# 56 constant matmuls for 30, and another order of the opening, in a kernel of chunk-selected attention and a gated FFN

## The chip, the cores and the metric

The kernel runs on one core of a Trainium2 chip. The metric is the device time of one execution in microseconds (us), lower is better. The engines are named as the profile names them: PE is TensorE's matmuls and PEld its weight loads, DVE is VectorE, ACT is ScalarE, POOL is GpSimd, and SP is the sync engine, which here only issues DMAs.

## The reference

Attention comes first: 4 batches, 8 heads, 768 positions, head size 64. The keys of a head are cut into 24 chunks of 32. For each query and chunk an upper bound is the sum over the head's dimensions of the larger of q times the chunk's minimum and q times its maximum. Each query keeps its six chunks with the highest bound among those that causality allows, and takes a softmax over the causal positions in them. The result is laid out as 3072 tokens of 512 values and goes through a gated feed-forward part with 1536 inner columns.

```python
k_min, k_max = min and max of k over each chunk of 32
ub = sum_d max(q * k_min, q * k_max)           # causal chunks only
top_chunks = argsort(ub)[..., -6:]
scores = q @ k.T / sqrt(64)                    # selected chunks, causal
x = softmax(scores) @ v                        # 3072 x 512
out = (sigmoid(x @ w_gate) * (x @ w_val)) @ w_out
```

## The kernel before

The 3072 tokens are worked in eight units u0 to u7 of three blocks of 128 tokens, 384 columns each. Unit u0 holds the first block of batches 0, 1 and 2; the others hold later blocks. In a first block no chunk has to be chosen, so it goes the short way of the function `first`.

Nothing is scheduled at run time. Every piece of work is put into a plan under a name (`plan.add`), and `Plan.order` replays a string written out by hand, `ORDER`: `kfT_0=P` means that the piece kfT_0 comes next and runs on TensorE (P), and A, V, G and S stand for ScalarE, VectorE, GpSimd and SP. So the string gives both the engine of each piece and the order on each engine. `SLOTS` says which buffer of a kind each tile takes (eight PSUM banks; six "v" buffers for what SP loads first), and `TIES` adds waits between two pieces that share no data. A piece waits only for its data, its buffer and its ties.

The names that matter below, with the unit or block as a suffix:

- `fl_i` (L591, in `keep_awake`): a constant matmul, ones times ones, 128x128 by 256 columns; nothing reads its result. L595 makes 30 of them.
- `kf`, `qf`, `vf` of blocks 0, 1 and 2 are loaded by SP in the function `load_first` (L631, L636). All of them take "v" buffers, so the later ones wait until an earlier one has been read. `kq_u1` is the load of unit u1 (L647).
- `kfT`, `qfT` (L709): the four transposes of a block's keys or queries; `kf16`, `qf16` copy the result to fp16. `scf` (L746): the scores of a block, eight matmuls. `expf` (L751, ScalarE): exponential, one for each half of the heads. `cmf` (L753, GpSimd): causal mask. `pvf` (L760): product with the values, `v16` or `vh` (cast by `vc` on GpSimd). `rzf`, `xf` (L766, L768, VectorE): division by the sum. `xpsf` (L775) turns the result back and `xTf` copies it into `xT_u0`, from which the FFN reads.
- `kn`, `qn` copy the keys and queries of u1 out of their load, `kT`, `qT` (L795) turn them, `kt`, `hk`, `hq`, `qf`, `qm`, `kx`, `kcr` prepare the selection from them, `ub_u1` (L896) computes its bounds.
- `epat` (L566, GpSimd) is a mask pattern for the selection, and the eight `hkp` copies spread it over the rows of the key tiles that hold no keys, 64x1536 values each. Before, three of them are on ScalarE (110, 000, 111), three on VectorE (001, 011, 101), two on GpSimd (010, 100).
- `wgp`, `wg0` to `wg2`, `wv0` to `wv2` (L610 to L613) and `wo0` to `wo2` (L618): the weights in thirds, their DMAs issued by GpSimd. `wgp` is the first quarter of the first third of w_gate, `wg0` the rest of it.
- `g_u0_fb`, `v_u0_fb` (both L1259): gate and value products of unit u0 for 128 inner columns, four matmuls each. fb 0 to 3 read the first third of the weights, 4 to 7 the second, 8 to 11 the last. `g_u0_0` needs all of `xT_u0`.

The hand-over to the later work is smooth: the first score tiles of u1 (`sc_u1`, L957) stand behind the first value products of u0 in TensorE's order, and from there attention of one unit and FFN of the one before alternate.

Of the kernel before, what the change touches and what calls it, by code (L numbers as in the profile page):

```python
# [116 lines left out]
tanh_u0_6=A g_u0_7=P tanh_u0_7=A hg_u0_7=V v16_0_1=G cm_u1_3=G pv_u1_3=P cm_u1_2=G hk1_u1_1=G g_u0_4=P tanh_u0_4=A hg_u0_4=V
vf1_3=G hq1_u1_2=G pv_u1_2=P sc_u1_5_1=P sc_u1_4_2=P sc_u1_4_1=P rz_u1_1=V x_u1_1=V exp_u1_4_1=A v_u0_9=P v_u0_10=P xps_u1_1=P
xT_u1_1=A exp_u1_4_2=A hg_u0_6=V hk1_u1_3=V hg_u0_5=V v_u0_8=P g_u0_10=P tanh_u0_10=A kcr1=V hg_u0_10=V g_u0_8=P tanh_u0_8=A
hg_u0_8=V sc_u1_5_2=P exp_u1_5_2=A g_u0_9=P tanh_u0_9=A hg_u0_9=V sc_u1_4_0=P exp_u1_4_0=A cm_u1_1=G pv_u1_1=P cm_u1_0=G qn_u2_2=G  # L120
sc_u1_5_0=P pv_u1_0=P exp_u1_5_0=A sc_u1_6_1=P exp_u1_6_1=A sc_u1_6_2=P exp_u1_6_2=A exp_u1_5_1=A sc_u1_7_2=P sc_u1_7_0=P
g_u0_11=P qT_u2_2=P sc_u1_7_1=P tanh_u0_11=A exp_u1_7_2=A exp_u1_7_0=A exp_u1_7_1=A kn_u2_1=V kT_u2_1=P rz_u1_0=V x_u1_0=V
xps_u1_0=P cm_u1_5=G pv_u1_5=P cm_u1_4=G pv_u1_4=P qf_u2_2=V q1_u2=S qn_u2_1=V qT_u2_1=P sc_u1_6_0=P kt_u2_1=A exp_u1_6_0=A
kn_u2_0=G kT_u2_0=P kt_u2_0=A v_u0_11=P rz_u1_2=V xT_u1_0=V x_u1_2=V xps_u1_2=P q3_u2=S qn_u2_3=G qT_u2_3=P cm_u1_7=G pv_u1_7=P
kx0_u2_0=V o0_u0_0=P o1_u0_0=P hg_u0_11=V kx1_u2_1=V kx1_u2_0=V cm_u1_6=G pv_u1_6=P rz_u1_3=V x_u1_3=V q0_u2=S qn_u2_0=A qT_u2_0=P
o0_u0_1=P xps_u1_3=P xT_u1_3=V qf_u2_1=A hq0_u2_2=A qf_u2_3=A qm_u2_1=G hq1_u2_1=G k2_u2=S kn_u2_2=G hk1_u2_0=A xT_u1_2=A
kT_u2_2=P k3_u2=S kn_u2_3=A kT_u2_3=P qf_u2_0=V hq0_u2_1=G hq0_u2_0=G qm_u2_0=G hk0_u2_1=G o2_u0_0=P osb_u0_0=A hq1_u2_0=A
qm_u2_2=A qf0_3=S qfT_3=P o1_u0_1=P o2_u0_1=P vf_3=S kf1_3=S kf0_3=S kfT_3=P v_0_5=S v_0_4=S kx0_u2_1=V kx0_u2_3=V kx1_u2_3=V
# [1328 lines left out]
```

## Time and profile before

| what | value |
|---|---|
| runs | 282.29, 280.89 and 280.53 us, median 280.89 |
| profiled execution | 279.88 us, its span 278.2 us |
| busy share of the span | PE 97%, DVE 83%, ACT 65%, POOL 59% |
| moved by DMA | 34.70 MB, mean 125 GB/s |
| granted TensorE clock over the span | 1.00 |

The span runs from the first to the last instruction; some 1.7 us of the execution lie outside it. In the timelines a row is a run of instructions of one kind on one engine: start, length, line, operation, output and inputs, count, and in brackets the idle time before it with what ended it. In the list of waits the numbers are the microseconds in total, how often, and the longest. In the table by stage each engine has its busy time and, in brackets, its number of instructions.

### The profile page before, as it was taken

How to read it: one execution, taken by the hardware profiler on the slowest of the kernel's cores; microseconds unless marked ns; L12 is line 12 of the kernel's file. 1: busy time of each engine (PE TensorE's matmuls, PEld its weight loads, DVE VectorE, ACT ScalarE, POOL GpSimd, SP SyncE). 2: the span in 40 equal slices, each digit the busy share in tenths (PEclk: the TensorE clock that was granted, in tenths of full speed). 3: DMA queues.
4: the chain of work that ended last, by engine and by line, in shares of the span. 5: the costliest groups of instructions: out<-in, count | busy, mean ns of one | idle time of the engine just before them, and what ended most of it. 6: DMA issues, size and time to landing. Idle time of an engine off the chain costs nothing.

```text
span 278.2 us, 7566 instructions
## 1 busy us (share of the span) xinstructions
PE 269.2 (97%) x2806; PEld 189.3 (68%) x2806; DVE 231.2 (83%) x686; ACT 180.4 (65%) x386; POOL 163.1 (59%) x262
## 2 busy tenths in 40 slices
PE   5979999999999999999999999999999999999995
PEld 3755658667755666557687657776888688778684
DVE  4799747687999998796999987978889998888985
ACT  6388969569858944468689979988983422341430
POOL 5797744639372873534669966724766467163440
PEclk9999999999999999999999999999999999999999
DMA  6999999999999598696896230100320033000304
GB/s 157 258 281 204 207 217 208 220 179 202 187 217 189 142 183 188 145 161 125 164 157 114 68 85 17 40 0 3 73 77 2 1 83 127 2 1 2 151 2 152
DMA packets 131717, 34.70 MB, mean 125 GB/s; under 512 B 119776, under 2 KB 128736, under 8 KB 131680
## 3 DMA queue, kind: packets, MB, share of 16 engines
q1 hardware_dynamic: 126912, 29.50, 50.6%
...
## 4 chain that ended last, share of the span: by engine, by line
PE 87%; DMA 6%; DVE 5%; SPq 1%; issue 0%; POOL 0%; DVEq 0%
PE v_u L1259 20%; PE g_u L1259 15%; PE sc_u L957 12%; PE o_u L1308 11%; PE p_u L1082 10%; PE pv_u L990 7%; DMA wg<-in_moe_w_gate_dram 5%; PE p_g_u L1191 5%; PE ube_u L896 3%; DMA kf<-in_k_dram 1%; DVE xf L768 1%; PE kfT L709 1%; PE qfT L709 1%; PE fl L591 1%; DVE kx_u L681 1%; DVE kcr L681 1%
## 5 line engine op out<-in xcount | busy, mean ns | idle before, releaser
L968 ACT ACTIVATE att_u<-sc_u 128x512 f16<-128x512 f32 (+3 forms) x184 | 86.9, 573 | 8.6 <-PE sc_u L957 7.3
L1259 PE MATMUL v_u<-xT_u,wv 128*128 128x384 f16 x384 | 72.4, 326 | 0.0
L1280 DVE SCALAR_TENSOR_TENSOR hg_u<-gate_u,v_u 128x384 f16<-128x384 f16 x96 | 51.2, 545 | 19.3 <-ACT gate_u L1271 9.7
L1271 ACT ACTIVATE gate_u<-g_u 128x384 f16<-128x384 f32 x72 | 35.1, 499 | 40.3 <-PE g_u L1259 35.1
L1259 PE MATMUL g_u<-xT_u,wg 128*128 128x384 f16 x288 | 56.0, 326 | 0.9 <-ACT xT_u L452 0.5
L1259 PEld LDWEIGHTS <-wv 128*128 128x128 f16 x384 | 36.2, 98 | 20.3 <-issue 0.2
L974 POOL TENSOR_SCALAR_AFFINE_SELECT att_u<-att_u 128x384 f16<-128x384 f16 (+1 forms) x56 | 28.0, 509 | 37.4 <-ACT att_u L968 16.4
L1259 PEld LDWEIGHTS <-wg 128*128 128x128 f16 x288 | 26.7, 98 | 18.3 <-DMA wg<-in_moe_w_gate_dram 1.8
L1308 PE MATMUL o_u<-wo,hg_u 128*128 128x512 f16 x144 | 34.3, 379 | 0.0
L990 PE MATMUL pv_u<-v,att_u 128*128 128x65 f16 x640 | 26.3, 193 | 0.0
L990 PEld LDWEIGHTS <-att_u 128*128 128x128 f16 x640 | 24.2, 98 | 2.9 <-issue 0.6
L1228 DVE TENSOR_TENSOR f_g_u<-p_g_u,f_g_u 128x192 f32<-128x192 f32 (+1 forms) x72 | 24.9, 383 | 1.0 <-PE p_g_u L1191 0.4
L957 PE MATMUL sc_u<-hqe,hke 128*128 128x128 f16 (+2 forms) x220 | 25.1, 243 | 0.0
L957 PE MATMUL sc_u<-hqo,hko 128*128 128x128 f16 (+2 forms) x220 | 24.1, 243 | 0.0
L1308 PEld LDWEIGHTS <-hg_u 128*128 128x128 f16 x144 | 13.7, 98 | 13.4
L957 PEld LDWEIGHTS <-hke 128*128 128x128 f16 x220 | 16.5, 98 | 4.9 <-issue 0.6
L957 PEld LDWEIGHTS <-hko 128*128 128x128 f16 x220 | 16.4, 98 | 4.4
L673 POOL CAST v<-v 128x512 f16<-128x512 f32 x23 | 14.4, 627 | 5.8 <-DVE qf_u L863 1.8
L1271 ACT ACTIVATE gate_u<-f_g_u 128x384 f16<-128x384 f32 x24 | 11.9, 519 | 5.6 <-DVE hg_u L1280 2.9
L1011 DVE TENSOR_TENSOR x_u<-pv_u,rz_u 128x384 f16<-128x384 f32 (+1 forms) x28 | 14.6, 524 | 0.9 <-DMA xT_u<-x_u 0.6
L919 DVE MAX8 mx_u<-ubn_u 128x8 f32<-128x8 f32 (+16 forms) x152 | 12.7, 158 | 0.3
L1099 DVE SCALAR_TENSOR_TENSOR sw<-p_u,sw 128x256 f32<-128x256 f32 (+1 forms) x20 | 10.6, 528 | 2.4 <-PE p_u L1082 2.0
...
## 6 DMA issues: line engine op xcount, KB each, us to landing
...
k<-in_k_dram SPq DMA_DIRECT2D x12, 384.0 KB, 5.4
q<-in_q_dram SPq DMA_DIRECT2D x12, 384.0 KB, 5.9
...
wv<-in_moe_w_val_dram POOLq DMA_DIRECT2D x3, 512.0 KB, 9.8
wo<-in_moe_w_out_dram POOLq DMA_DIRECT2D x3, 512.0 KB, 17.6
qf<-in_q_dram SPq DMA_DIRECT2D x8, 128.0 KB, 3.3
```

The costliest lines, as they stand in the source:

```text
L673: plan.add(f"v16_{b}_{ib}", {POOL: pool(H * D)}, lambda e: nc.gpsimd.tensor_copy(v16[b % 2][:, ib, :, 0:D], at(t)), reads=[t], writes=[("v ...
L957: nc.tensor.matmul(at(t)[:, o:o + 128 * m], hk[b % 2][e_][:, p, 128 * jb:128 * jb + 128], hq[u.side][e_][:, p, 128 * x:128 * (x + m)], sta ...
L968: plan.add(f"exp_{u.name}_{h}_{y}", {ACT: act(n)}, lambda e, t=t, att=att, b0=b0, n=n: nc.scalar.activation(at(att)[:, b0:b0 + n], at(t), ...
L974: nc.gpsimd.affine_select(out=dv, in_=dv, compare_op=ALU.is_ge, fill=0.0, base=0, pattern=[[0, u.m], [1, 128]], channel_multiplier=-1)
L990: nc.tensor.matmul(at(pv)[:, last, x, :], at(att)[:, c:c + 128], v16[b % 2][:, jb, h, :], start=(jb == 0), stop=(jb == ib))
L1011: plan.add(f"x_{u.name}_{p}", {DVE: dve(u.t)}, lambda e: nc.vector.tensor_tensor(at(x_).rearrange("p a (e d) -> p e a d", e=2), at(pv)[:, ...
L1082: nc.tensor.matmul(at(to)[:, side], a(j)[:, i], b(j)[:, i], start=j == i == 0, stop=j == 2 and i == 1)
L1228: plan.add(f"{p}_{name}", {POOL: pool2(192 * n), DVE: dve(192 * n)} if slow else {DVE: dve(192 * n)}, lambda e: both(e).tensor_tensor(dst( ...
L1259: nc.tensor.matmul(at(t), w16[:, c, 128 * fb:128 * fb + 128], at(u.xt)[:, c, :], start=(c == 0), stop=(c == 3))
L1271: plan.add(f"tanh_{u.name}_{fb}", {ACT: act(T, not seven[0])}, lambda e, gv=gv, gate=gate: nc.scalar.activation(at(gate), gv(), AF.Tanh, s ...
L1280: plan.add(f"hg_{u.name}_{fb}", {DVE: dve(T)}, lambda e, vv=vv, gate=gate, hg=hg, fb=fb: nc.vector.scalar_tensor_tensor(at(hg)[:, fb % 2], ...
L1308: nc.tensor.matmul(at(o), at(hgs[fc // 2])[:, fc % 2, 128 * tb:128 * tb + 128], wo16[:, fc, lo:hi], start=(fc == 0), stop=(fc == NFB - 1))
```

## The change

The loop makes 56 constant matmuls for 30. The string `ORDER` is another one ahead of `sc_u1_3_0`; from there on, 1765 pieces stand in the same order on the same engines. In the new part

- 32 constant matmuls stand on TensorE ahead of `kfT_0`, where 9 stood, and `kT_u1_2` comes behind `kfT_0`;
- `scf_1` stands behind `pvf_0_1`, and `scf_2` behind `pvf_1_0`;
- four pattern copies are on ScalarE (011, 010, 000, 001), three on VectorE (100, 110, 101), one on GpSimd (111);
- `hkf0` goes from GpSimd to ScalarE, some casts and copies of u1 change their engine, and `cmf_2_0` comes ahead of `wv0` on GpSimd;
- SP issues its 128 DMAs in the same order as before.

Six ties are new. `SLOTS` names other PSUM banks and other buffers of equal kind in much of the kernel; the later pieces keep their waits but for a few that wait for another of the banks just freed.

```diff
--- before.py
+++ after.py
@@ ORDER: all up to the common rest @@
-ident=G ones16=V fl_4=P fl_2=P fl_8=P fl_3=P fl_1=P fl_0=P fl_29=P k2_u1=S kn_u1_2=A qf1_0=S kf1_0=S kf0_0=S fl_6=P fl_5=P epat0=V
-ident16=V ap0=V epat=G hkp110=A hkp000=A hkp001=V kT_u1_2=P kcr0=V kt_u1_2=V hk0_u1_2=G vf1_1=G hkp011=V hkp010=G vf1_2=G hkp100=G
-kf1_2=S kf0_1=S kfT_0=P kxf1=V fl_17=P fl_10=P fl_7=P kx0_u1_2=V kf16_0=V qf0_0=S qfT_0=P qf16_0=V qf1_1=S kf1_1=S kfT_1=P
-kf16_1=V fl_15=P fl_16=P scf_0=P expf_0_1=A fl_19=P qf0_1=S qfT_1=P hq0=V ap1=V fl_14=P fl_9=P fl_13=P fl_11=P fl_18=P fl_12=P
-qf16_1=V scf_1=P v10=G vf_0=S v16_0_0=G qf0_2=S qf1_2=S kf0_2=S expf_0_0=A cmf_0_0=G pvf_0_0=P rzf_0_0=V xf_0_0=V kx1_u1_2=V
-cmf_0_1=G wgp=G kfT_2=P pvf_0_1=P qfT_2=P qf16_2=V rzf_0_1=V xf_0_1=V kxf0=V expf_1_0=A cmf_1_0=G vf_1=S vc_1=G pvf_1_0=P
-rzf_1_0=V xpsf_0_0=P expf_1_1=A cmf_1_1=G pvf_1_1=P hkf0=G hk1_u1_2=A kf16_2=A scf_2=P expf_2_1=A expf_2_0=A k0_u1=S kn_u1_0=V
-kT_u1_0=P xf_1_0=V fl_20=P fl_21=P wg0=G q3_u1=S qn_u1_3=A q2_u1=S rzf_1_1=V xf_1_1=V xpsf_1_1=P hq1=V xTf_1_1=V kx0_u1_0=V
-kx1_u1_0=V vf_2=S wv0=G cmf_2_0=G fl_23=P xpsf_0_1=P fl_24=P fl_22=P fl_27=P xpsf_1_0=P vc_2=G xTf_1_0=V pvf_2_0=P rzf_2_0=V
-xf_2_0=V q1_u1=S k3_u1=S kn_u1_3=G kT_u1_3=P hkp111=A q0_u1=S fl_28=P kx1_u1_3=V cmf_2_1=G pvf_2_1=P xpsf_2_0=P rzf_2_1=V xf_2_1=V
-qT_u1_3=P qf_u1_3=V k1_u1=S qn_u1_1=A qT_u1_1=P xTf_0_0=A xTf_0_1=A qn_u1_2=A qn_u1_0=A kn_u1_1=G kT_u1_1=P kx1_u1_1=V kx0_u1_1=V
-kt_u1_0=A qm_u1_3=A fl_25=P xpsf_2_1=P fl_26=P qT_u1_2=P v_0_3=S v_0_2=S v_0_1=S qf1_3=S k0_u2=S q2_u2=S k1_u2=S qf_u1_1=V
-qf_u1_2=V v11=G wv1=G wg1=G hq0_u1_3=G qT_u1_0=P kt_u1_3=A hk0_u1_3=G hq1_u1_3=G wv2=G xTf_2_1=A xTf_2_0=A qf_u1_0=A qm_u1_0=A
-g_u0_0=P g_u0_2=P kx0_u1_3=V kcr_f=V kcr_u1=V hkp101=V hq1_u1_0=V hkf1=V kt_u1_1=V hk0_u1_1=G wg2=G qm_u1_2=A qm_u1_1=A ub_u1=P
-ubn0_u1=V ubm0_u1=V hq0_u1_1=A hq0_u1_2=A g_u0_3=P g_u0_1=P mx0_u1=V ap0_u1=V apt0_u1=V hqm0_u1_0=V v_u0_1=P v_u0_0=P v_u0_2=P
-hq0_u1_0=A tanh_u0_2=A tanh_u0_1=A hg_u0_1=V ubn1_u1=V v_u0_3=P tanh_u0_3=A hg_u0_3=V ubm1_u1=V hg_u0_2=V tanh_u0_0=A hg_u0_0=V
-hk0_u1_0=A hq1_u1_1=A sc_u1_0_2=P exp_u1_0_2=A sc_u1_1_2=P sc_u1_0_1=P sc_u1_0_0=P exp_u1_1_2=A sc_u1_1_0=P sc_u1_1_1=P
-exp_u1_0_0=A exp_u1_0_1=A v_u0_7=P wo0=G hqm0_u1_2=G sc_u1_2_2=P exp_u1_2_2=A sc_u1_2_0=P exp_u1_2_0=A
+ident=G vf1_1=G ones16=V fl_2=P fl_15=P fl_34=P k2_u1=S hq1=V epat0=V epat=G hkp111=G hkp100=V hkp011=A hkp010=A ident16=V qf1_0=S
+kf1_0=S kf0_0=S fl_8=P fl_19=P fl_53=P fl_28=P fl_10=P fl_32=P fl_40=P fl_30=P fl_13=P fl_48=P fl_26=P fl_27=P fl_31=P fl_33=P
+fl_3=P fl_5=P fl_6=P fl_0=P fl_37=P fl_4=P fl_41=P fl_17=P fl_12=P fl_50=P fl_9=P fl_35=P fl_54=P fl_45=P fl_29=P kfT_0=P
+kn_u1_2=V fl_24=P fl_47=P kT_u1_2=P v10=G hkp000=A kf1_2=S kf0_1=S qf0_0=S qfT_0=P qf16_0=A qf1_1=S kf1_1=S fl_11=P fl_46=P
+fl_23=P fl_51=P qf0_1=S kfT_1=P kf16_0=V kcr0=V fl_18=P scf_0=P fl_7=P fl_43=P fl_38=P qfT_1=P fl_16=P fl_1=P hkp110=V kxf1=V
+qf16_1=V vf_0=S v16_0_0=G qf0_2=S qf1_2=S kt_u1_2=A hk0_u1_2=G expf_0_0=A cmf_0_0=G fl_21=P fl_36=P fl_44=P pvf_0_0=P rzf_0_0=V
+xf_0_0=V kx0_u1_2=V qfT_2=P qf16_2=V fl_14=P fl_52=P xpsf_0_0=P expf_0_1=A vf1_2=G cmf_0_1=G pvf_0_1=P kf16_1=A scf_1=P expf_1_0=A
+kf0_2=S fl_22=P rzf_0_1=V ap0=V kfT_2=P kf16_2=V ap1=V xf_0_1=V xTf_0_0=V fl_25=P fl_39=P fl_20=P wgp=G vf_1=S vc_1=G expf_1_1=A
+hkp001=A cmf_1_0=G pvf_1_0=P scf_2=P expf_2_0=A cmf_1_1=G pvf_1_1=P rzf_1_1=V k0_u1=S kn_u1_0=V kT_u1_0=P wg0=G q3_u1=S q2_u1=S
+fl_42=P vf_2=S cmf_2_0=G wv0=G qn_u1_3=A qT_u1_3=P xf_1_1=V xpsf_1_1=P expf_2_1=A rzf_1_0=V xf_1_0=V kxf0=V xpsf_1_0=P xpsf_0_1=P
+vc_2=A pvf_2_0=P qf_u1_3=A qm_u1_3=A q1_u1=S k3_u1=S kn_u1_3=V kT_u1_3=P q0_u1=S rzf_2_0=V xf_2_0=V hkf0=A xpsf_2_0=P xTf_2_0=A
+qn_u1_1=A xTf_0_1=A cmf_2_1=G pvf_2_1=P fl_55=P kx1_u1_2=V qT_u1_1=P xTf_1_1=A k1_u1=S v_0_3=S v_0_2=S v_0_1=S qf1_3=S k0_u2=S
+q2_u2=S k1_u2=S qn_u1_0=G qT_u1_0=P fl_49=P kn_u1_1=G kT_u1_1=P kt_u1_1=A qn_u1_2=G wv1=G wg1=G wv2=G rzf_2_1=V xf_2_1=V qT_u1_2=P
+qf_u1_2=A qf_u1_1=A qm_u1_2=G kcr_f=G qf_u1_0=A hq1_u1_3=A qm_u1_0=A kx0_u1_3=V kx0_u1_0=V kt_u1_3=V kx1_u1_3=V xTf_1_0=V
+xpsf_2_1=P xTf_2_1=V g_u0_0=P g_u0_2=P kx1_u1_0=V kx0_u1_1=V kx1_u1_1=V kcr_u1=V hkp101=V hk0_u1_1=V hkf1=V hq0_u1_2=V wg2=G
+qm_u1_1=A hk1_u1_2=A ub_u1=P ubn0_u1=V ubm0_u1=V mx0_u1=V kt_u1_0=A hq0_u1_0=G v11=G g_u0_1=P g_u0_3=P ap0_u1=V hq1_u1_0=V
+apt0_u1=V hqm0_u1_0=V hq0=V v_u0_1=P tanh_u0_1=A hg_u0_1=V ubn1_u1=V v_u0_3=P v_u0_0=P v_u0_2=P tanh_u0_3=A hg_u0_3=V ubm1_u1=V
+tanh_u0_2=A hg_u0_2=V tanh_u0_0=A hq0_u1_1=A hg_u0_0=V hk0_u1_0=A hq1_u1_1=A sc_u1_0_2=P exp_u1_0_2=A sc_u1_1_2=P sc_u1_0_1=P
+sc_u1_0_0=P exp_u1_1_2=A sc_u1_1_0=P sc_u1_1_1=P exp_u1_0_0=A exp_u1_0_1=A v_u0_7=P wo0=G hq0_u1_3=G hqm0_u1_2=G sc_u1_2_2=P
+exp_u1_2_2=A sc_u1_2_0=P exp_u1_2_0=A hk0_u1_3=G
 sc_u1_3_0=P ...
@@ SLOTS: the constant matmuls and the renamed banks @@
-epat:0 fl_0:5 fl_1:4 fl_2:1 fl_3:3 fl_4:0 fl_5:0 fl_6:7 fl_7:5 fl_8:2 fl_9:6 fl_10:4 fl_11:3 fl_12:6 fl_13:7 fl_14:3 fl_15:0
...
+epat:0 fl_0:4 fl_1:5 fl_2:0 fl_3:1 fl_4:6 fl_5:2 fl_6:3 fl_7:1 fl_8:3 fl_9:3 fl_10:7 fl_11:5 fl_12:1 fl_13:3 fl_14:5 fl_15:1
...
@@ TIES: six more, the others as they were @@
+hkp111<epat0 qn_u1_0<rzf_2_0 kn_u1_1<xf_2_0 qn_u1_2<kx1_u1_2 qm_u1_2<xf_2_1 hq0_u1_0<hq0_u1_2
...
-    for i in range(30):
+    for i in range(56):
         keep_awake(i)
```

More of the change, by code (lines that the diff above doesn't have):

```diff
@@ L117 @@
[L117 to L128, printed above, removed]
@@ L264 @@
+c21_u7=V out_u7_1=S out_u7_0=S held_u6_5=A p2z_u67=P p6_u67=P p6z_u67=P p5_u67=P p5z_u67=P c11_u67=V u4_u67=V sw3_u67_2=G
+sw3_u67_1=G p3_u67=P p3z_u67=P c12_u67=V out_u67_0=S sw2_u67_2=G p7_u67=P p7z_u67=P c22_u67=V out_u67_b1=S p4_u67=P p4z_u67=P
+c21_u67=V out_u67_1=S
 """
 SLOTS = """
[L267 to L268 removed]
@@ L269 @@
-vf_0:5 kf_1:3 qf_1:4 vf_1:0 kf_2:2 qf_2:1 vf_2:3 kq_u1:0 v_0_1:2 v_0_2:5 v_0_3:4 kfT_0:2 kf16_0:3 kx_f:0 qfT_0:6 qf16_0:4
-scf_0_0:4 scf_0_1:5 attf_0_0:1 pvf_0_0:5 rzf_0_0:0 xf_0_0:0 xpsf_0_0:5 xT_u0:0 attf_0_1:2 pvf_0_1:6 rzf_0_1:1 xf_0_1:1 xpsf_0_1:1
-kfT_1:7 kf16_1:5 qfT_1:0 qf16_1:6 vh_1:1 scf_1_0:7 scf_1_1:3 attf_1_0:3 pvf_1_0:7 rzf_1_0:0 xf_1_0:2 xpsf_1_0:7 attf_1_1:1
-pvf_1_1:3 rzf_1_1:1 xf_1_1:0 xpsf_1_1:0 kfT_2:4 kf16_2:4 qfT_2:0 qf16_2:0 vh_2:2 scf_2_0:1 scf_2_1:0 attf_2_0:3 pvf_2_0:0
@@ new lines @@
+kq_u1:0 v_0_1:1 v_0_2:5 v_0_3:4 kfT_0:0 kf16_0:3 kx_f:0 qfT_0:4 qf16_0:2 scf_0_0:6 scf_0_1:7 attf_0_0:1 pvf_0_0:6 rzf_0_0:0
+xf_0_0:0 xpsf_0_0:5 xT_u0:0 attf_0_1:2 pvf_0_1:7 rzf_0_1:1 xf_0_1:1 xpsf_0_1:2 kfT_1:2 kf16_1:1 qfT_1:1 qf16_1:4 vh_1:0 scf_1_0:2
+scf_1_1:6 attf_1_0:3 pvf_1_0:2 rzf_1_0:1 xf_1_0:0 xpsf_1_0:5 attf_1_1:1 pvf_1_1:1 rzf_1_1:0 xf_1_1:2 xpsf_1_1:1 kfT_2:1 kf16_2:2
+qfT_2:4 qf16_2:5 vh_2:6 scf_2_0:6 scf_2_1:4 attf_2_0:2 pvf_2_0:4 rzf_2_0:0 xf_2_0:2 xpsf_2_0:6 attf_2_1:3 pvf_2_1:4 rzf_2_1:1
@@ new lines @@
+xf_2_1:0 xpsf_2_1:2 kn_u1_0:1 kT_u1_0:7 kx_u1:1 kt_u1_0:0 kn_u1_1:1 kT_u1_1:1 kt_u1_1:1 kn_u1_2:1 kT_u1_2:3 kt_u1_2:0 kn_u1_3:2
+kT_u1_3:0 kt_u1_3:2 qn_u1_0:0 qT_u1_0:6 qf_u1:0 qm_u1:0 qn_u1_1:5 qT_u1_1:3 qn_u1_2:4 qT_u1_2:4 qn_u1_3:4 qT_u1_3:6 ube_u1:2
+ubo_u1:4 ubn_u1:0 mx_u1:0 apt_u1:0 g_u0_0:0 gate_u0_0:0 v_u0_0:2 hg_u0_0:0 g_u0_1:3 gate_u0_1:2 v_u0_1:1 g_u0_2:5 gate_u0_2:1
+v_u0_2:3 hg_u0_1:1 g_u0_3:6 gate_u0_3:3 v_u0_3:7 g_u0_4:6 gate_u0_4:0 v_u0_4:5 hg_u0_2:3 g_u0_5:4 gate_u0_5:2 v_u0_5:2 g_u0_6:1
@@ new lines @@
+k16_2_3<kx0_2_0 v16_2_0<hg_u2_0 k16_2_1<rz_u3_3 hk0_2_0<x_u3_1 v16_2_1<qf1_u4_0 hq0_u4_2<qm_u4_2 hq0_u4_0<qf0_u6_1
+hq1_u4_0<qf0_u6_3 kcr_2<hg_u2_11 hk0_2_2<mx1_u4 cm_u4_1<qf0_u5_2 cm_u4_2<hg_u3_0 k16_3_2<qf0_u6_2 qm_u5_2<k16_3_0 cm_u4_7<kt_3_1
+cm_u4_3<hqm0_u5_0 cm_u4_5<rz_u4_0 hq0_u5_2<hg_u3_6 v16_2_2<hg_u3_7 v16_2_4<rz_u4_1 hqm0_u5_2<x_u4_1 cm_u4_6<kx0_3_2
+hk0_3_1<rz_u4_2 cm_u5_0<x_u4_2 k16_3_3<rz_u4_3 hqm1_u5_0<x_u4_3 v16_3_0<qf1_u6_2 hqm1_u5_2<rz_u5_0 cm_u5_3<qf1_u6_3 hk1_3_1<kt_3_3
+hq0_u7_2<hk0_3_3 cm_u5_5<qf0_u7_1 v16_3_2<x_u5_1 hq0_u7_0<ubn1_u6 hqm1_u6_2<hqm1_u6_0 v16_2_5<rz_u5_2 cm_u6_3<x_u5_2
```

476 lines of the change are left out of this document (239 added, 237 removed).

## The prediction

> **What bounds the kernel now.** First the page, for the share of each engine and the chain that ended last.
>
> ```profile
> PE 269.2 (97%) x2806; PEld 189.3 (68%) x2806; DVE 231.2 (83%) x686; ACT 180.4 (65%) x386; POOL 163.1 (59%) x262
> PEclk9999999999999999999999999999999999999999
> DMA  6999999999999598696896230100320033000304
> PE 87%; DMA 6%; DVE 5%; SPq 1%; issue 0%; POOL 0%; DVEq 0%
> ```
>
> TensorE is busy in 97% of the span, so nearly everything it must do sets the end, and only its idle time or its useless work can be won. The DMA row is full in the first 13 of 40 slices: during the change's part of the kernel, something else runs at its limit too. The second view is TensorE's waits, the third the chain of waits.
>
> ```profile
> PE fl L591 <- DVE ones L587: 1.1, 1, 1.1
> PE pvf L760 <- POOL vh L456: 1.0, 2, 0.8
> PE kfT L709 <- DMA kf<-in_k_dram: 0.9, 1, 0.9
> PE kT_u L795 <- POOL epat L566: 0.8, 1, 0.8
> PE g_u L1259 <- ACT xT_u L452: 0.5, 1, 0.5
> PE g_u L1259 <- DMA wg<-in_moe_w_gate_dram: 0.2, 1, 0.2
> ```
> ```profile
> 26.18 14.22 DMA wg<-in_moe_w_gate_dram
> 40.45 1.48 PE g_u L1259 x8
> ```
>
> These six waits make 4.5 us of the whole execution, and every one lies before 40.5 us. The chain says more than the length of a wait does: the last thing it finds ahead of TensorE's unbroken run is no work of the opening but the third part of w_gate, issued at 26.18 and landed at 26.18 + 14.22 = 40.40. TensorE stood ready only 0.25 us earlier. So 40.40 is a meeting point of two streams, and the change touches both: TensorE's opening and the time at which GpSimd issues the weights. To know how close they run I read the traffic by stage, then the landings of single weight parts.
>
> ```profile
> 5.00:10.00 5.00, 4.19 (x21) 3.02 (x23) 3.84 (x7) 1.78 (x2) 4.12 (x7) 1.00 1.07 241
> 15.00:20.00 5.00, 3.72 (x47) 2.53 (x46) 4.65 (x16) 3.85 (x8) 4.85 (x9) 1.00 1.19 292
> 20.00:25.00 5.00, 4.37 (x48) 2.95 (x52) 4.92 (x14) 4.92 (x14) 4.05 (x8) 1.00 1.22 204
> 35.00:40.00 5.00, 5.00 (x49) 3.07 (x46) 2.56 (x7) 3.19 (x8) 1.32 (x4) 1.00 1.20 217
> ```
> ```profile
> wg<-in_moe_w_gate_dram POOLq DMA_DIRECT2D x1, 384.0 KB, 7.3
> wg<-in_moe_w_gate_dram POOLq DMA_DIRECT2D x1, 128.0 KB, 5.5
> wv<-in_moe_w_val_dram POOLq DMA_DIRECT2D x3, 512.0 KB, 9.8
> ```
>
> The columns after PE, PEld, DVE, ACT and POOL busy are clock, DMA share and GB/s. The DMA share stays above 1 from 5 us on, while TensorE loses 0.81 us in 5–10, 1.28 in 15–20 and 0.63 in 20–25, and nothing in 35–40. VectorE and ScalarE are both at 4.92 of 5 us just ahead of the gate products. The DMA rows give KB and us from issue to landing: of w_gate the rest of the first part (wg0) and its first quarter (wgp), of w_val the median of three.
>
> **The opening, instruction by instruction.** The timeline of TensorE:
>
> ```profile
> 1.12 2.10 PE L591 MATMUL fl<-ones 128*128 128x256 f16 x9 [1.12 <-DVE ones L587]
> 5.81 1.09 PE L709 MATMUL kfT<-ident,kf 128*128 128x128 f32 x4 [0.90 <-DMA kf<-in_k_dram]
> 8.40 1.08 PE L709 MATMUL kfT<-ident,kf 128*128 128x128 f32 x4
> 9.85 0.61 PE L746 MATMUL scf<-qf,kf 64*128 64x128 f16 x8
> 10.39 0.40 PE L591 MATMUL fl<-ones 128*128 128x256 f16 x1
> 11.43 1.01 PE L591 MATMUL fl<-ones 128*128 128x256 f16 x6
> 12.43 0.40 PE L746 MATMUL scf<-qf,kf 64*128 64x128 f16 x8
> 12.89 0.63 PE L709 MATMUL kfT<-ident,kf 128*128 128x128 f32 x4
> 13.36 0.29 PE L760 MATMUL pvf<-v,attf 128*128 128x65 f16 x4
> 17.65 0.27 PE L591 MATMUL fl<-ones 128*128 128x256 f16 x1
> 17.87 0.49 PE L591 MATMUL fl<-ones 128*128 128x256 f16 x3
> 22.82 1.76 PE L1259 MATMUL g_u<-xT_u,wg 128*128 128x384 f16 x8 [0.51 <-ACT xT_u L452]
> 40.45 1.48 PE L1259 MATMUL g_u<-xT_u,wg 128*128 128x384 f16 x8 [0.25 <-DMA wg<-in_moe_w_gate_dram]
> ```
>
> The PEclk row shows 9 everywhere, yet a constant matmul takes 0.40 us alone at 10.39 and 0.27 at 17.65. Nine in a row give (2.10 - 0.40)/8 = 0.21 us each, three later ones (0.49 - 0.27)/2 = 0.11. Four transposes take 1.08 us at 8.40 and 0.63 at 12.89. So TensorE starts at half speed and changes inside the six of 11.43: 1.01 - 0.27 = 0.74 for five steps is about two slow and three fast, hence near 11.8, which is 3.4 us after 8.40, the start of its first gapless stretch.
>
> **The change part by part, in TensorE's time.**
> *The constant matmuls.* In place of 9 ahead of kfT_0 there are 32, then 17 ahead of the second scores (12 before) and 7 behind them (9 before). If 3.4 us of gapless work from 1.12 bring the full clock at 4.5, 16 run at 0.21 and 16 at 0.11: 3.4 + 1.8 = 5.2, and kfT_0 starts at 6.3. If no grant comes, 32 x 0.2125 = 6.8, at 7.9. Before it was 5.81, so kfT_0 is 0.5 to 2.1 late.
> *The clock.* With the grant in hand the work between kfT_0 and the second scores runs fast: four groups of transposes at 1.09 - 0.63 = 0.46 less, the first scores at 0.61 - 0.40 = 0.2 less, that is up to 2.0 us. It covers the late start in the one case and most of it in the other. First scores: 9.85 - 2.0 + (0.5 to 2.1) = 8.4 to 10.0.
>
> The Trainium skill ("TensorE: Matmul & The Clock Gate", Part 1: The HAM clock gate) says that the clock watches a free-running window of about 3.4 us, not a number of matmuls. By it the 3.4 us of the rows agree, the grant may fall anywhere between the two cases above, and a matmul beyond it is time spent for nothing.
>
> *The first weights.* GpSimd issues wgp behind the two masks of the first scores, both before and after.
>
> ```profile
> 7.91 1.46 POOL L456 COPY hke<-epat 64x1536 f16<-64x1536 f16 x1
> 11.65 1.22 POOL L753 TENSOR_SCALAR_AFFINE_SELECT attf<-attf 128x512 f16<-128x512 f16 x2 [1.19 <-ACT attf L751]
> 12.82 0.79 POOL L610 DMA_DIRECT2D wg<-in_moe_w_gate_dram  x1
> 15.35 0.61 POOL L456 COPY hke<-kf 64x512 f16<-64x512 f16 x1
> 15.91 0.80 POOL L612 DMA_DIRECT2D wg<-in_moe_w_gate_dram  x1
> ```
>
> wgp went out 12.82 - 9.85 = 3.0 us behind the first scores, and GpSimd had waited 1.19 us for the exponential, so its pattern copies (1.46 us) were hidden: taking one away brings nothing here. The new order puts hk0_u1_2 (0.61, as hke<-kf) and a memset between the masks: +0.6 at most, 0 if they fit a wait. wgp then goes out at 11.4 to 13.6, a shift of -1.4 to +0.8; nearest to the middle, -0.2, as the copies between (0.7 us each, unchanged by the clock) recover only part of the 2.0.
> wg0 loses the 0.61 of hkf0 ahead of it, but the second scores now stand behind pvf_0_1, which needs exponential, mask and cast of the first: 13.36 - 9.85 = 3.5 behind the first scores, so 11.9 to 13.5 against 12.43, -0.5 to +1.1, less 0.6: wg0 at 14.8 to 16.4 against 15.91. It does not matter: wgp lands at 12.82 + 5.5 = 18.3, so wg0 is queued behind it in either case, and wv0, now behind one more mask (0.65), is queued before wg0 lands at 15.91 + 7.3 = 23.2. The last part, wg2, is issued some 2 us sooner than 26.18, but it had 14.22 us in the queue; its issue is not what dates it. Five of the six new ties make GpSimd copies wait for VectorE or for each other; behind them on GpSimd stand wv1, wg1, wv2 and wg2. Covered too: a w_val part needs 9.8 us from issue to landing, most of it in the queue. So the weight stream moves with wgp or less, -1.4 to +0.8, and since loads of both queues keep the share above 1, I take half of -0.2: -0.1.
>
> *SP's loads.* Its order is the same, but qf of the third block waits until kfT_0 frees a buffer.
>
> ```profile
> 6.93 1.43 SPq L636 DMA_DIRECT2D qf<-in_q_dram  x2
> ```
>
> This goes out 6.93 - 5.81 = 1.1 behind kfT_0: at 7.4 to 9.0. What is in flight then covers the first half us; a hole of up to 1.6 us can open. I take +0.2 for the stream, bounds 0 and +0.9 (half of 1.6, and a little for the loads behind).
>
> *Pattern copies to ScalarE, other small copies.*
>
> ```profile
> 5.32 1.47 ACT L452 COPY hke<-epat 64x1536 f16<-64x1536 f16 x1
> 16.20 1.08 ACT L751 ACTIVATE attf<-scf 128x512 f16<-128x512 f32 x2 [1.12 <-PE scf L746]
> ```
>
> Three of ScalarE's four copies fall early, where it was idle (1.78 of 5 us busy in 5–10): 0, and 1.5 each if a first exponential had to wait for one. The fourth, hkp001, now stands ahead of the third block's exponentials, where ScalarE waited 1.12: 1.47 - 1.12 = 0.35 late, and behind it the masks, pvf_2 and the last xT_u. VectorE keeps three. Ahead of g_u0_0 both are full, and the same copies are dealt out anew; the last xT_u now comes from VectorE, behind three reductions. I take +0.2 us for g_u0_0, bounds -0.3 and +0.6 (the 0.35 and one small copy, or one small copy less). It can hardly gain: its second matmul needs wg0 at 23.2, and the first group at 22.82 shows that, 1.76 us for eight where 1.48 is usual.
>
> *The sum.* TensorE is ready for the third w_gate part at 40.45 - 0.25 + 0.2 = 40.4. The part lands at 40.40 - 0.1 + 0.2 = 40.5. The later of the two, plus the 0.05 that lay between landing and start, is 40.55 against 40.45: +0.1. Bounds: earliest -0.4 (TensorE 39.9, stream 39.0, and TensorE decides at 40.05), latest +1.7 (stream +0.8 and +0.9). Behind that the orders and waits are kept; I read a few other PSUM banks as 0, with +-0.3. The profiled execution took 279.88 us, 278.2 of span and 1.7 around it, and becomes 280.0. It stood 1.0 under the median of the runs, 280.89, so my forecast for a median is 281.0.
>
> **The rivals.**
> *Faster by 1% and more.* The stream is paced by its own start, not by the engines: 292 GB/s in 15–20 against 204 in 20–25 shows room. wgp goes out 1.4 sooner, kq and vf loads end sooner, and all six waits but those for ones and kf go (4.5 - 2.0 = 2.5). With the 0.3 that I left to VectorE that is -2.8: 278.1. Against it: the gate products would have to begin at 20, where VectorE and ScalarE have 4.92 of 5 us of work in front of them.
> The Trainium skill ("DMA: Bandwidth & Descriptors", Queues, rings and completion order) has each DMA engine take the queues in turn, packet by packet; by it an earlier weight queue would take its turns from SP's loads, and gain less than its own lead. The full share of the rows fits that.
>
> *Slower.* SP's loads. The clock is granted late, kfT_0 starts at 7.9, qf goes out at 9.0 and the queue runs dry for the 2.1 us: every later k, q, v and weight lands 2.1 later, and wg2 at 42.5: 282.9. It decides from a kfT_0 later than about 6.6. For it: TensorE's queue holds kfT_0, not the data. Against: several loads are outstanding and share 1.07.
>
> *The clock is lost again,* so the change does not do what it says. Behind the second scores 7 constant matmuls stand for 9, and TensorE was idle 1.28 us of 15–20 already. Half speed for 3.4 us from 22.82 costs 1.7, less nothing: TensorE at 42.1, 282.6. Against: the earlier start leaves the waits much as they were.
>
> **How the numbers follow.** The likeliest, no change that can be told, 0.50: own range 280.3 to 282.6. Faster rival 0.17; slower rival 0.20; clock lost 0.13. A measurement of this kernel tells about 1%, 2.8 us, from no change. The faster case lies at it or beyond; the two slower ones reach it in about six of ten, when their price meets the stream's own +0.9: 0.20. That leaves 0.17 faster, 0.63 within, 0.20 slower. The range takes in the slower cases to 283.3 and the faster one down to 278.6, short of its end.
>
> **What would show it.** Right: in the profile after, constant matmuls turning to 0.11 us steps between 4.5 and 8 us, kfT_0 at 6.3 to 7.9, wgp issued within 1 us of 12.8, the first gate product near 23, and the third w_gate part landing within 1 us of 40.4, with TensorE at most 0.5 us early or late. Wrong: that landing moved by over 2 us; a TensorE wait over 0.5 us behind 41 us; transposes of 1.08 us per four behind 9 us; or a span moved although the third part's first product is where it was.

## Result and the profile after

The changed kernel took 283.37 us in the median of 20 runs (280.81 to 285.51), the kernel before 281.14 (280.13 to 285.21). The ratio is 1.0072, 95% interval 1.0051 to 1.0092: 2.0 us slower. Runs more than 1.5% above the fastest of their kernel are left out of the ratios: two of these 20, and one of the 20 before. Twenty runs resolve less than the 1% of the forecast, so within "no change that can be told" there is a loss to explain. The profiled execution took 283.25 us, close to the median, and its span is 281.5 against 278.2. The profiled execution of before (279.88) was faster than each of its 20 runs here, so the two profiles lie 1.1 us further apart than the medians do. From the page after, the share of each engine, the clock, and the chain that ended last:

```profile
PE 272.8 (97%) x2832; PEld 191.8 (68%) x2832; DVE 231.2 (82%) x685; ACT 183.7 (65%) x388; POOL 162.2 (58%) x261
PEclk9997999999999999999999999999999999999999
PE 88%; DMA 5%; DVE 4%; SPq 1%; issue 1%; ACT 0%; DVEq 0%
```

TensorE is busy 3.6 us longer, and in the fourth slice (21 to 28 us) the clock is not full. TensorE's waits after, then two pieces of the chain of waits:

```profile
PE kT_u L799 <- DVE kn_u L458: 2.6, 2, 1.8
PE fl L595 <- DVE ones L591: 1.1, 1, 1.1
PE pvf L764 <- POOL attf L757: 0.4, 1, 0.4
```
```profile
1.12 5.38 PE fl L595 x32
13.09 6.63 DMA kq_u<-in_k_dram
```

The third part of w_gate has left the chain. A load of u1's keys stands there instead: `k3_u1`, issued at 13.09 and landed at 19.72. Between the two pieces the chain runs over `kfT_0`, the transposes behind it and SP's issues. TensorE's timeline after, from the opening to the meeting point at the third w_gate part:

```profile
1.12 5.38 PE L595 MATMUL fl<-ones 128*128 128x256 f16 x32 [1.12 <-DVE ones L591]
6.33 0.60 PE L713 MATMUL kfT<-ident,kf 128*128 128x128 f32 x4
16.66 0.55 PE L799 MATMUL kT_u<-ident,kn_u 128*128 128x128 f32 x3 [0.77 <-DVE kn_u L458]
20.36 0.55 PE L799 MATMUL kT_u<-ident,kn_u 128*128 128x128 f32 x3 [1.78 <-DVE kn_u L458]
22.07 1.54 PE L799 MATMUL qT_u<-ident,qn_u 128*128 128x128 f32 x6
25.11 1.70 PE L1263 MATMUL g_u<-xT_u,wg 128*128 128x384 f16 x8
43.50 1.46 PE L1263 MATMUL g_u<-xT_u,wg 128*128 128x384 f16 x8
```

The first gate product starts at 25.11 (before 22.82), the first that needs the third w_gate part at 43.50 (before 40.45): 3.05 of the 3.3 us by which the span grew. In between, six transposes take 1.54 us. VectorE and the two stages around this place, in the columns of the prediction's tables (the row of `kn_u1_3`, then the stages):

```profile
19.75 0.55 DVE L458 COPY kn_u<-kq_u 128x384 f32<-128x384 f32 x1 [1.67 <-DMA kq_u<-in_k_dram]
```
```profile
15.00:20.00 5.00, 2.60 (x33) 1.80 (x33) 3.27 (x11) 4.57 (x8) 3.25 (x5) 1.00 1.03 240
20.00:25.00 5.00, 4.23 (x24) 3.45 (x25) 3.94 (x11) 1.81 (x5) 3.68 (x6) 0.67 1.23 208
```

VectorE, which was busy 4.65 of 5 us in 15–20, is busy 3.27: `kn_u1_3` waits 1.67 us for its load at the head of VectorE's queue. TensorE is idle for 2.40 us in that stage and has 0.67 of its clock in the next. And the load is late although it was issued only 0.4 us later than before. In 14 to 16 us the queues moved, by the DMA view (packets, MB, share of 16 engines), before and then after:

```profile
q1 hardware_dynamic: 1317, 0.57, 103.5%
q0 software_dynamic: 31, 0.03, 10.6%
```
```profile
q1 hardware_dynamic: 907, 0.29, 73.4%
q0 software_dynamic: 47, 0.05, 16.5%
q8 instruction: 1, 0.02, 2.9%
```

SP's loads (q1) got 0.29 MB in place of 0.57, the weights (q0) 0.05 in place of 0.03. One packet of 16 KB is in that stage after, and not before: the queue named instruction, 2.9% of 16 engines in 2 us, which is 0.93 us on one engine. It starts at 15.58; before, that packet comes at 19.87. In the fourteen traces of this study (the two kernels and twelve more) it always comes when TensorE has issued 99 to 123 matmuls, with a weight load for each. So its place seems to go by the number of instructions, as for a block that TensorE reads ahead, and 26 more matmuls pull it forward by 4 us.

But the fall of SP's traffic is older than the packet. The same view of 14.5 to 15.5 us, before and then after:

```profile
q1 hardware_dynamic: 658, 0.30, 108.5%
q0 software_dynamic: 3, 0.00, 1.8%
```
```profile
q1 hardware_dynamic: 398, 0.13, 65.2%
q0 software_dynamic: 18, 0.02, 13.7%
```

Ahead of the packet SP's loads already move 0.13 MB for 0.30, and the DMA engines are not full (65.2% and 13.7% together). So the packet did not begin the fall. What did is not shown.

### The profile page after: what moved, and what is told of

The parts are those of the page before. It is cut to its first block, busy times and chain, and to the rows that moved or that the text cites. A ratio compares the mean times of both kernels' runs of the same rounds, so it can differ in the third digit from the quotient of the medians.

```text
span 281.5 us, 7624 instructions
## 1 busy us (share of the span) xinstructions
PE 272.8 (97%) x2832; PEld 191.8 (68%) x2832; DVE 231.2 (82%) x685; ACT 183.7 (65%) x388; POOL 162.2 (58%) x261
## 4 chain that ended last, share of the span: by engine, by line
PE 88%; DMA 5%; DVE 4%; SPq 1%; issue 1%; ACT 0%; DVEq 0%
PE v_u L1263 21%; PE g_u L1263 16%; PE sc_u L961 11%; PE o_u L1312 11%; PE p_u L1086 9%; PE pv_u L994 6%; PE p_g_u L1195 5%; PE ube_u L900 3%; DMA kq_u<-in_k_dram 2%; PE fl L595 2%; DMA xT_u<-x_u 2%; PE qT_u L799 1%; SPq L651 1%; PE kT_u L799 1%; DVE hg_u L1284 1%
## 5 line engine op out<-in xcount | busy, mean ns | idle before, releaser
L1312 PEld LDWEIGHTS <-hg_u 128*128 128x128 f16 x144 | 13.7, 98 | 13.4
```

Of the source, the lines that this page charges most:

```text
L1312: nc.tensor.matmul(at(o), at(hgs[fc // 2])[:, fc % 2, 128 * tb:128 * tb + 128], wo16[:, fc, lo:hi], start=(fc == 0), stop=(fc == NFB - 1))
```

## The experiments

The theories, in the order in which they came up: 1, the clock is lost at 20 us because TensorE is idle there, and that is the loss; 2, the late key load is, and the clock only follows; 3, the 32 constant matmuls hold `kfT_0`, and with it SP's loads that wait for a buffer; 4, the earlier read of instructions delays loads; 6, VectorE's queue behind `kn_u1_3` makes a late load dear. (The expectations use these numbers; there is no 5 among them.) Each kernel was timed in five rounds against the kernel before (281.1 us).

**Fill TensorE's waits.**

```diff
 ORDER of the changed kernel
+20 constant matmuls: 5 ahead of kT_u1_0, 12 ahead of kT_u1_3, 3 ahead of fl_55
```

> The changed kernel with 20 more constant matmuls put into TensorE's three longest waits between 15.9 and 21.7 us (5 ahead of kT_u1_0, 12 ahead of kT_u1_3, 3 ahead of the one behind pvf_2_1). Theory 1 (the clock is lost because TensorE stands idle there): the granted clock of the runs goes to 0.999 or 1.000, the eight first gate matmuls and the transposes ahead of them run at full speed again, and the time falls from 283.4 to 281.0 to 281.9. Theory 2 (the loss is the late key load in front of VectorE's queue, the clock only goes along with it): the clock may come back, but the time stays within 0.5 us of 283.4, since the waits for kn_u are as long as before.

284.47 us, ratio 1.0149 (1.0115 to 1.0183), clock 1.000 in four of six runs. The edit did more than was meant. TensorE's timeline:

```profile
18.91 3.85 PE L598 MATMUL fl<-ones 128*128 128x256 f16 x12
```

Twelve matmuls in the same PSUM bank took 3.85 us, 0.32 each, where they take 0.11 in different banks: they outlast the wait they were to fill. So this run does not separate theories 1 and 2; a fill that fits the waits stands further below. Whether the bank itself or a wait between two writers of one tile takes the 0.32 us is not shown.

**Nine ahead of `kfT_0`.**

```diff
 ORDER of the changed kernel
-fl_10=P ... fl_29=P        (23 of the 32 ahead of kfT_0=P)
```

> The changed kernel with 9 constant matmuls ahead of kfT_0 in place of 32; all else as changed. Theory 1 (clock lost at 20 us): the time stays at 283 to 284, since the idle stretch at 15 to 21 us is still there; the transposes of the opening run slow until about 9 us. Theory 3 (the 32 hold kfT_0, the loads behind it come late and all follows): kfT_0 starts near 5.8, the third block's queries are issued near 6.9, and the time falls to about 281.5.

281.07 us, ratio 0.9994 (0.9970 to 1.0019), and a mean clock of 1.000 in all twelve runs. The whole loss is gone with 23 constant matmuls. All the rest of the new order, its pattern copies included, costs nothing that can be told.

```profile
19.29 0.55 PE L796 MATMUL kT_u<-ident,kn_u 128*128 128x128 f32 x3 [0.27 <-DVE kn_u L455]
23.04 0.32 PE L1260 MATMUL g_u<-xT_u,wg 128*128 128x384 f16 x1 [0.29 <-DVE xT_u L455]
24.45 1.31 PE L1260 MATMUL g_u<-xT_u,wg 128*128 128x384 f16 x7 [1.09 <-DMA wg<-in_moe_w_gate_dram]
41.60 1.47 PE L1260 MATMUL g_u<-xT_u,wg 128*128 128x384 f16 x8 [0.19 <-DMA wg<-in_moe_w_gate_dram]
```

The wait for `kn_u1_3` is 0.27 in place of 1.78, and TensorE is back on the weights: at the first gate products and at the third part.

**The old order without its late constant matmuls.**

```diff
 ORDER of the kernel before
-fl_20=P fl_21=P fl_23=P fl_24=P fl_22=P fl_27=P fl_28=P fl_25=P fl_26=P
```

> The kernel before without the 9 constant matmuls that stand behind the second scores (16 to 21.5 us). Theory 1: TensorE's activity there falls under what holds the clock, the granted clock drops under 0.999 in a good part of the runs, and the time rises by 0.7 to 2 us, with a wider spread than the kernel before. Theory 2: the time stays at 281.1 within 0.3 us, since no load comes later.

281.18 us, ratio 1.0002 (0.9988 to 1.0015). Its page's clock, and TensorE's row at the third w_gate part:

```profile
PEclk9968999999999999999999999999999999999999
```
```profile
41.39 1.47 PE L1258 MATMUL g_u<-xT_u,wg 128*128 128x384 f16 x8 [0.61 <-DVE kcr L570]
```

The clock is lost in every run (0.987 or 0.988 in the eleven compared), as theory 1 said, and the time does not change: in the old order that half of theory 1 falls. With a lower clock in the third and fourth slice TensorE still stands 0.61 us ahead of the weights. (The row names VectorE, but the part had been issued at 27.28 and needed 14.1 us.)

**The old order with 32 ahead.**

```diff
 ORDER of the kernel before
+23 constant matmuls ahead of kfT_0=P
```

> The kernel before with 23 more constant matmuls ahead of kfT_0 (32 in all). Theory 3 (held loads): kfT_0 starts at 6.3 or later, the third block's queries are issued later by as much, and the time rises by 1 us or more. Theories 1 and 2: the time stays within 0.4 us of the kernel before; the full clock comes by 6 us and the opening up to 12 us is shorter, but the weights decide.

283.29 us, ratio 1.0083 (1.0062 to 1.0103). They stand behind `kT_u1_2`, which starts at 4.04, so they hold `kfT_0` for 3.5 us, more than the change does. TensorE's and SP's timelines:

```profile
9.32 0.66 PE L712 MATMUL kfT<-ident,kf 128*128 128x128 f32 x4
```
```profile
10.01 0.92 SPq L639 DMA_DIRECT2D qf<-in_q_dram  x2
```

The loads behind go out 3.1 us later than before (6.93) and the run is 2.2 us longer: the mechanism of theory 3 is real. (Its six runs have the clock lost as well, 0.987 to 0.994, and its read of instructions is at 17.45; neither costs as much in the old order alone, by the kernel above and by the one with 23 narrow matmuls below.) But in the changed kernel SP issues that load at 6.96, and with nine ahead at 7.21. Both theories 3 and 4 fit the time with nine ahead, so the next three separate the time that the constant matmuls take from their number.

**The same time in fewer instructions.**

```diff
 keep_awake, in the changed kernel
+        m = 4 if i in WIDE else 2
-        t = ps(f"fl_{i}", "pr", [128, 2, 128])
+        t = ps(f"fl_{i}", "pr", [128, m, 128])
 ORDER
-16 of the 32 ahead of kfT_0, 7 of the 17 up to scf_1 (the others of these pairs are WIDE)
```

> The changed kernel with its constant matmuls in the same places for the same time but in fewer instructions: each pair of 256 columns ahead of kfT_0, and seven pairs between it and the second scores, is one matmul of 512 columns (33 in all in place of 56). Theory 3 (the 32 hold kfT_0 and so the loads): no change, 283.0 to 283.6. Theory 4 (TensorE reads its instructions in blocks of 16 KB through one of the DMA engines; the 26 more matmuls pull the first block's read from 19.9 to 15.6 us, into the loads of u1's keys): the read goes back to 18.5 us or later, the third key load of u1 lands near 18.6, and the time falls to 280.8 to 281.5.

281.57 us, ratio 1.0019 (0.9990 to 1.0049). TensorE's and VectorE's timelines, and the DMA view of 18 to 19 us:

```profile
7.16 0.60 PE L713 MATMUL kfT<-ident,kf 128*128 128x128 f32 x4
```
```profile
18.93 0.55 DVE L455 COPY kn_u<-kq_u 128x384 f32<-128x384 f32 x1 [0.85 <-DMA kq_u<-in_k_dram]
```
```profile
q8 instruction: 1, 0.02, 6.0%
```

`kfT_0` starts even later (7.16), the read is at 18.7, the key load lands at 18.9, and 1.5 of the 2.0 us are back.

**The same instructions in less time.**

```diff
 keep_awake, in the changed kernel
+        if i in TINY:          # 23 of the 32 ahead of kfT_0
+            emit = lambda e: nc.tensor.matmul(at(t)[:, 0, 0:16], ones16, ones16[:, 0:16], start=True, stop=True)
```

> The changed kernel with all its 56 constant matmuls, but 23 of the 32 ahead of kfT_0 only 16 columns wide, so that they take little time and kfT_0 starts when its data is there (near 5.9). Theory 3: 280.8 to 281.5, as with 9 ahead. Theory 4: the block is read as early as in the changed kernel, at 15 to 16.5 us, and the time stays at 282.5 to 283.8.

282.56 us, ratio 1.0044 (1.0018 to 1.0069). `kfT_0` starts at 5.74, when its data is there, the read is at 14.9, and 1.2 us of the loss stay. With the last two, time and number make four cells:

| constant matmuls ahead of `kfT_0` | read at | ratio to before |
|---|---|---|
| few, short (9) | 19.8 | 0.9994 (0.9970 to 1.0019) |
| few, long (16 wide) | 18.7 | 1.0019 (0.9990 to 1.0049) |
| many, short (9 and 23 narrow) | 14.9 | 1.0044 (1.0018 to 1.0069) |
| many, long (the change) | 15.6 | 1.0072 (1.0051 to 1.0092) |

From the first row, length adds 0.25% of the time and number 0.50%, 0.7 and 1.4 us; together 0.75%, and 0.78% was measured. The intervals of the two middle rows overlap, so the split is only about that; that number counts without length is outside the noise of the third row. By what way it counts, the cells do not say.

**The old order with the same instructions.**

```diff
 ORDER of the kernel before
+23 constant matmuls of 16 columns ahead of kT_u1_2=P
```

> The kernel before with 23 constant matmuls of 16 columns more behind the nine leading ones: the instructions of the change without its hold of kfT_0 and without its order. Theory 4: the block is read near 15.5 to 16.5 us in place of 19.9, u1's key loads land 0.7 to 1.5 us later, and the time rises by 0.5 to 2 us. Theory 3: no change, 281.1 within 0.3 us.

281.45 us, ratio 1.0010 (0.9986 to 1.0034), the read at 16.3. Theory 4 expected 0.5 to 2 us and got 0.3, within noise: the early read by itself costs little here. The same instructions do cost in the new order.

**`kn_u1_3` off VectorE.**

```diff
 ORDER of the changed kernel
-kn_u1_3=V kT_u1_3=P ... cmf_2_1=G pvf_2_1=P
+... cmf_2_1=G kn_u1_3=G kT_u1_3=P pvf_2_1=P
```

> The changed kernel with kn_u1_3 on GpSimd behind cmf_2_1 in place of VectorE, and kT_u1_3 ahead of pvf_2_1. Theory 6 (the late key load costs because kn_u1_3 waits for it at the head of VectorE's queue, 1.67 us, with rzf_2_0 and all behind it waiting too): VectorE's wait is gone and the time falls to 282.2 or less. If the loss lies in the clock or in the hold of kfT_0 instead, the time stays at 283.0 to 283.6.

282.59 us, ratio 1.0025 (0.9993 to 1.0057). The median of all twelve lies between the two outcomes named, that of the nine compared is 281.85, under the 282.2 of theory 6. Part of the price seems to lie in VectorE's queue, but the interval reaches to the changed kernel's. The profiled execution took 285.65 us and is not read here.

**Fill the waits without outlasting them.**

```diff
 ORDER of the changed kernel (512 columns each, banks in turn)
+fl_56=P fl_57=P kT_u1_0=P
+fl_58=P fl_59=P fl_60=P fl_61=P kT_u1_3=P
```

> The changed kernel with six constant matmuls of 512 columns in TensorE's two longest waits, two (0.4 us) ahead of kT_u1_0 and four (0.9 us) ahead of kT_u1_3, in alternating banks so that they do not wait for one another; the first read of instructions stays at 15 to 16 us. Theory 1 (the lost clock is the larger part): nearly all runs at a granted clock of 0.998 or more and a median of 281.0 to 282.0. Theory 4 with the late key load as the larger part: the clock comes back, the median stays at 282.4 to 283.4.

283.18 us, ratio 1.0041 (1.0004 to 1.0078), and a clock of 0.998 or more in ten of the eleven runs compared. Those ten still have a median of 282.7. Of the changed kernel's own runs, the 6 with that clock have 281.4 and the other 12 have 283.8, which looks like a cause; but with the clock restored the time is not. The kernel before says the same: by that mark its clock is lost in 50 of its 92 compared runs, with a median only 0.05 to 0.53 us longer in the three sets of runs timed beside these kernels. So theory 1 is unlikely as the larger part; it is not excluded, since the fill adds work of its own. The timeline shows what came in its place:

```profile
18.60 1.06 PE L599 MATMUL fl<-ones 128*128 128x512 f16 x4
43.03 1.47 PE L1267 MATMUL g_u<-xT_u,wg 128*128 128x384 f16 x8 [0.55 <-DMA wg<-in_moe_w_gate_dram]
```

Here TensorE waits for the third w_gate part, 2.6 us late against 40.45.

**More instructions still.**

```diff
 ORDER and keep_awake, in the changed kernel
-32 constant matmuls of 256 columns ahead of kfT_0
+6 of 512 and 80 of 16 columns
```

> The changed kernel with 86 constant matmuls ahead of kfT_0 in place of 32, six of 512 columns and 80 of 16, in about the same time (5 to 6.5 us). Theory 4: it is the place of the read among the loads that costs, not the number of instructions: the first block is read at 8 to 11 us, the third key load of u1 lands near 18.6 again, and the median falls to 281 to 282.3. If more instructions cost by themselves, the median is 283.4 or more.

282.70 us, ratio 1.0043 (1.0014 to 1.0073), runs from 282.1 to 283.9. The read fell at 12.5, not at 8 to 11, and so still among the loads; the load of `kn_u1_3` took 4.3 us (before 5.8), and the first w_gate part was late:

```profile
25.28 1.31 PE L1277 MATMUL g_u<-xT_u,wg 128*128 128x384 f16 x7 [1.11 <-DMA wg<-in_moe_w_gate_dram]
```

The median missed the expectation by 0.4 us. Nine of the twelve runs have the clock at 0.998 or more and a median of 282.9: again a kept clock with the loss. The loss does not grow with the number of instructions (54 more, and no more than the change), but that an early enough read would be free is not shown.

**The key load first.**

```diff
 ORDER of the changed kernel
-q3_u1=S q2_u1=S ... vf_2=S ... q1_u1=S k3_u1=S
+q3_u1=S k3_u1=S q2_u1=S ... vf_2=S ... q1_u1=S
```

> The changed kernel with SP issuing the load for kn_u1_3 ahead of three others (q2_u1, vf_2, q1_u1). Theory 4 and 6 together (the read delays this load, and VectorE stands behind it): kn_u1_3 is not waited for any more, the median falls to 281.2 to 282.2. If the loss lies in the clock or in another load: 282.7 or more, vf_2 being later by about 0.5 us.

283.13 us, ratio 1.0059 (1.0024 to 1.0095): no gain. ScalarE's and TensorE's timelines:

```profile
19.00 0.62 ACT L456 CAST vh<-vf 128x512 f16<-128x512 f32 x1 [1.35 <-DMA vf<-in_v_dram]
```
```profile
19.68 0.38 PE L764 MATMUL pvf<-vh,attf 128*128 128x65 f16 x4 [1.59 <-ACT vh L456]
```

Nobody waits for `kn_u1_3`; now vf_2 is the late load, and TensorE waits 1.59 us for it in the same place. It landed 1.4 us later than in the changed kernel, at 19.0, and 0.8 of that is the edit's own: SP issues it at 12.26, not at 11.50. The 16 KB packet was at 13.7 and took 12.0% of 16 engines in one us, 1.9 us of one engine. So the loss is not tied to this one load, or to VectorE's place for it.

**Wide constant matmuls and the key load first.**

```diff
 the edits of the two kernels above (same time in fewer instructions; the key load first)
```

> The 33 wide constant matmuls and the earlier load for kn_u1_3 together, a candidate for beating both kernels. Theory 4: the waits left in the run with wide matmuls (1.8 us for kn_u) shrink to 0.8, the median falls under 281.1, to 280.3 to 281.0. If the third w_gate part decides as before: 281.0 to 281.5.

281.79 us, ratio 1.0022 (0.9982 to 1.0062): not under the kernel before. None of the twelve is, beyond the noise. ScalarE's timeline:

```profile
18.11 0.62 ACT L453 CAST vh<-vf 128x512 f16<-128x512 f32 x1 [0.41 <-DMA vf<-in_v_dram]
```

SP issues vf_2 at 12.29, as in the kernel above (12.26), and with 23 constant matmuls fewer it lands 0.9 us sooner.

## Why the prediction was right, and where it was not

The forecast was 281.0 and no change that 1% can tell. The measured ratio lies within that 1%; the direction of the small rest, +0.72%, was given by two rivals and not by the sum. From the 280.89 that the forecast starts at, the ratio makes 282.9: above the likeliest case's own 280.3 to 282.6, and inside the range to 283.3 that takes in the slower cases. So that no change came out is in part luck: the mechanism was not the one of the sum. Two of the signs named for it failed, the first gate product near 23 (25.11) and TensorE at most 0.5 us from the landing of the third part (2.6 us behind it). The sum's lower bound has a slip: with TensorE at 39.9 it is 39.95 and -0.5, not 40.05 and -0.4. The result lies at the other end.

- *The constant matmuls and the clock.* Right. Thirty-two in 5.38 us are about 17 slow and 14 fast steps, so the clock came near 4.7, and `kfT_0` at 6.33 is the early end of 6.3 to 7.9. In the other profiles with 32 of them at the start it lay between 6.1 and 7.5: the change of clock does not come at the same place in each execution. The Trainium skill ("TensorE: Matmul & The Clock Gate", Part 1: The HAM clock gate) says so too: the window that the clock goes by does not start with the kernel, so the change comes sooner or later from run to run.
- *The first weights.* Right. The views of GpSimd after:

```profile
12.29 0.79 POOL L614 DMA_DIRECT2D wg<-in_moe_w_gate_dram  x1
15.42 0.80 POOL L616 DMA_DIRECT2D wg<-in_moe_w_gate_dram  x1
26.89 0.84 POOL L616 DMA_DIRECT2D wg<-in_moe_w_gate_dram  x1
```

  wgp went out 0.5 early and wg0 inside its bounds. The last part left 0.7 later than before, not 2 earlier, and landed 14.0 us behind its issue, at 40.9 for the forecast 40.5: its issue indeed does not date it.
- *SP's loads.* The change in the profiled execution was 0.03 us, better than the 7.4 to 9.0 given: `kfT_0` is 0.5 later, but its transposes take 0.60 for 1.09. Over many executions the hold is worth about 0.5 to 0.7 us (the wide row of the table, whose interval reaches to no loss at all), inside the 0 to +0.9 given. As a rival it was given 2.0 for a hole of 2.1; the old order with 32 ahead shows 2.2 for a hole of 3.1.
- *The first gate product: the step that failed.* "I take +0.2 us for g_u0_0, bounds -0.3 and +0.6" was 2.29. With nine ahead of `kfT_0` the same order begins it at 23.04, +0.22, and then waits for wg0: what I had priced, the order and its copies, came out as priced in that trace. The rest comes with the 23 constant matmuls. I took the loads that feed the copies of u1 to land when they had. In the trace of before these loads had no slack, by two rows that the prediction's list of waits leaves out and the timeline row of `kT_u1_3`:

```profile
PE kT_u L795 <- DVE kn_u L454: 0.5, 1, 0.5
PE kT_u L795 <- POOL kn_u L456: 0.2, 1, 0.2
19.20 0.55 PE L795 MATMUL kT_u<-ident,kn_u 128*128 128x128 f32 x3 [0.16 <-POOL kn_u L456]
```

  And the new order moves `kn_u1_3` from GpSimd into VectorE's queue, with the divisions of the attention behind it. A load late by 1.2 us (19.7 for 18.5) stops VectorE for 1.67 and TensorE for 1.78; the rest to 2.29 is 22.07 to 25.11 at a lower clock.
- *What the sum left out* is that constant matmuls cost by their number too. I priced them in TensorE's time alone. The table gives the number about 0.50% (1.4 us) in this order; in the old one nothing can be told. That the way is the read of instructions is argued, not shown: its packet stood in the trace of before at 19.87, behind the loads, and stands among them where there is a loss by number.
  The Trainium skill ("Runtime: NRT & Kernel Launch", Instruction fetch mechanics) says that each engine's instructions are refilled in blocks of 16 KiB, 256 instructions, by a DMA queue of the engine's own, and that the cost of a block is mostly hidden. The traces agree on the size and fit the number (99 to 123 matmuls, each with a weight load, ahead of the first read). On the cost they show 0.93 us of one DMA engine for the packet, and leave open what of the 0.50% is its doing.
- *The clock-lost rival.* It happened in 12 of the 18 runs compared, but in the kernel before it happens in 50 of 92, so the change did little to how often. By itself it cost little: one kernel has the clock lost in all runs and no loss of time, two (the second fill, and more instructions still) have it kept in most runs and most of the loss still there. Why the changed kernel's runs without it are 2.4 us faster than those with it is not taken apart.
- *The meeting point.* Read rightly, and it decides how much the opening may slip unpaid: 0.25 us. Everything beyond that was paid in full, 3.05 at 43.50 and 3.3 at the end. In twelve of the fourteen profiled executions 239.4 to 240.1 us pass from the start of this product to the end of the execution (240.8 and 242.2 in the others), so its start dates the whole kernel. Against nine ahead, whose profile is no faster than its median (281.36 us, 41.60), the change is 1.90 later, about the loss.

What stays open: how the number of instructions costs. Against the packet as the whole answer stand the fall of SP's traffic ahead of it; the load of `kn_u1_3`, which took 4.3 to 6.6 us in the seven traces with SP's order kept and the read at 12.5 to 16.3, and 5.3 to 5.8 in the four with the read at 18.7 to 19.9 (6.6 with 32 ahead in the old order, where the read is at 17.45); the same early read in the old order, which cost nothing that can be told; and 54 more instructions, which cost no more. The records do not say on which of the 16 engines a packet ran, and each trace is one execution. The spread of the changed kernel (281 to 285.5 us, 280 to 282 for most runs of before) is also not explained; with 23 narrow matmuls the runs at a clock of 0.998 or more still spread from 281.1 to 284.0. A read placed ahead of all loads was not reached.
